# DeltaNet and a multiplicative FFN on one core: two more units' w1/w2 products from eleven half products, with the order of the second half written anew

## The chip, the core and the metric

The kernel runs on one core of a Trainium2 chip: TensorE (PE, matmuls into PSUM), VectorE (DVE), ScalarE (ACT), GpSimd (POOL) and SyncE (SP, which issues the DMAs). The metric is device time in microseconds, the median of several executions.

## The reference, cut to what matters

```python
# attention: q, k, v of (4, 8, 768, 48), beta of (4, 8, 768)
k_n = k / (norm(k) + 1e-06)
for t in range(768):
    y[t]  = q[t] @ state
    state = state + beta[t] * outer(k_n[t], v[t] - state.T @ k_n[t])
x = y as (4 * 768, 8 * 48)                   # 3072 tokens of 384 features
# ffn: w1, w2 of (384, 1024), w3 of (1024, 1024), w_out of (1024, 384)
out = (((x @ w1) * (x @ w2)) @ w3) @ w_out
```

All of it is float32.

## The kernel before, in words

The 768 positions are cut into 12 chunks of 64. Two chunks of all four batches, 512 tokens, are a **unit**; there are six, u = 0 to 5, and "the fourth unit" is u = 3. The delta rule is solved chunk by chunk: scores (step names `s`), the inverse of a triangular 32 x 32 block for every head (`V`, one run for two chunks), the corner that joins two such blocks (`e`), the state chain (`c`) and the outputs (`y`), which write the unit's transposed token features into the tile xT. The FFN folds w3 @ w_out once into one matrix w34. After that a unit has two stages: `a`, the products with w1 and w2 and their elementwise product, and `o`/`x`, the product with w34 and the results.

Nothing is scheduled by the machine: the table ORDER names one step after the other, each step is a piece of a generator (up to its next `yield`), and every engine executes its instructions in exactly that order. `a32` is a step of unit 3's pair (or slab) 2, `V4` one of the inverse for chunks 8 and 9, `S3` the sums over unit 3's slabs, `W` sums over w1 and w2, `X4` sums over unit 4's tokens, `n` and `g` GpSimd work on values and keys, `p` and `d` the loads and transposes of keys and queries, `N` the norms, `u` the write of a chunk's block to DRAM from which V loads it.

**Stage a of units 0 to 4** (`ab`, line 927): for each 128 of the 1024 FFN features, a **slab** of 128 x 512, three matmuls of 512 columns with w1 (384 features are 3 times 128), a copy to SBUF on ScalarE, three with w2, a multiplication on VectorE that reads the second product from PSUM.

**Stage a of the last unit, u = 5** (`features`, line 1055): two slabs at a time, as a **pair** p = 0 to 3, with 256 tokens per half. The 2 x 2 block scheme of Strassen and Winograd, with [w1 w2] as one operand and the unit's token halves as the other, needs seven products in place of eight for two thirds of the features; the last third takes four plain ones. That makes eleven products, each two matmuls of 256 columns (`onto`, one per slab of the pair), where the plain way has twelve of that size. They accumulate in four PSUM banks, ps_a to ps_d. ScalarE copies four intermediate sums out (into `first`, `tmp`, Y0, Y1), VectorE adds a bank to each of these four (line 1083), and Y0 \*= first and Y1 \*= tmp end the pair (lines 1118 and 1131): on VectorE for the last unit, on GpSimd for any other. Two sums over weights (T2, T3, T4 and a new w2, made by `W`, line 1020) and four over tokens (`X`, line 1043, on GpSimd) come first.

**Stage o** (`o`, line 1143) works on token halves and feature halves in seven blocks; between them GpSimd forms sums of the slabs in place (`slab_sums`, line 992).

**The inverse** (`inverse`, line 497) has 31 steps of two VectorE instructions, each on what the one before wrote: tb = V's column times U's row (line 524), V -= tb (line 529). From the third run on, V, U and tb all lie in SBUF.

PSUM banks are handed out in turn (`bank`, four of them): the fifth request gets the first again and its writer waits for that bank's last reader.

Of the kernel before, what the change touches and what calls it, by code (L numbers as in the profile page):

```python
# [45 lines left out]
P17 P17 f5 f5 V0 V0 f1 V0 V0 P17 t8 P15 V0 h0 V0 V0 P14 f5 P26 t6 P23 P20 V0 q2 P27 k2 t6 t9 t14
t9 v0 V0 P23 f4 f4 t14 f4 t15 t15 P21 P15 P15 t7 q3 V0 v1 Q2 Q2 V0 e0 h0 h0 e0 Q2 g1 e0 g1 t7 g1
f3 e0 e0 K2 P27 K2 e1 e0 e0 n0 e1 k3 f7 P27 n0 e1 c0 e1 P21 e1 f7 V1 g1 c0 y0 P28 c0 P20 P25 f7
P20 P20 P29 f3 P33 y0 n1 n1 P21 g1 c0 c1 y0 g1 g1 K2 f3 P28 P28 P28 P34 c1 t13 t13 t12 t12 P25
P27 K3 K3 K3 e1 s2 g1 P25 P29 P35 g1 P25 P33 f6 f6 P29 P29 e1 g1 N1 Q3 Q3 c1 y0 s2 s2 s2 P34 c1  # L50
s2 s2 f6 Q3 s3 K2 P30 P34 P34 P26 P26 P24 y1 y1 s3 P30 P31 N1 P33 N1 s3 b6 b6 P33 P35 P35 u2 P35
# [1307 lines left out]
```

## Time and profile before

| | before |
|---|---|
| time, median of 3 (us) | 558.43 (557.59 to 558.78) |
| span of the profiled execution (us) | 556.1 |
| granted TensorE clock | 1.000 |
| TensorE busy (us, share of the span) | 533.6 (96%) |
| VectorE busy | 343.7 (62%) |
| GpSimd busy | 169.7 (31%) |
| ScalarE busy | 145.7 (26%) |

The page gives the profiled execution by its span, from the first instruction to the last; the time of a whole execution is not given for it and lies 2.3 us higher in the median. A matmul in float32 leaves two records. A line number belongs to the kernel before; in the changed kernel the same code stands 10 to 16 lines lower. A group's row has the line, engine, operation, tiles and count, then busy us and mean ns, then the idle time before it and who ended it.

### The profile page before, as it was taken

The page shows a single profiled execution, that of the slowest core. Times are in us where ns is not written, and L with a number is a line of the kernel's source. Part 1 is how long each engine was busy: PE and PEld are TensorE (multiplying, and loading weights), DVE is VectorE, ACT ScalarE, POOL GpSimd, SP SyncE. Part 2 cuts the span into 40 slices and gives each one's busy share as a digit, 9 for nine tenths or more (in the row PEclk, how much of TensorE's full clock was granted, in tenths as well). Part 3 has the DMA queues.
Part 4 walks back from the last instruction along what each step waited for, and adds up shares of the span by engine and source line. Part 5 has one row for each costly group of instructions (what it writes and reads, how often), then busy time and mean ns, then how long its engine had stood idle before and what let it go on. Part 6 is the DMA issues. An engine that isn't in the chain of part 4 may idle for free.

```text
span 556.1 us, 19932 instructions
## 1 busy us (share of the span) xinstructions
PE 533.6 (96%) x8732; PEld 390.8 (70%) x8732; DVE 343.7 (62%) x800; ACT 145.7 (26%) x291; POOL 169.7 (31%) x213
## 2 busy tenths in 40 slices
...
GB/s 189 339 307 230 158 140 150 128 160 55 96 48 55 119 147 72 67 88 89 122 74 100 70 91 80 126 38 83 51 15 154 26 60 38 18 58 1 0 2 57
DMA packets 191527, 54.22 MB, mean 98 GB/s; under 512 B 178928, under 2 KB 185072, under 8 KB 191440
## 3 DMA queue, kind: packets, MB, share of 16 engines
...
q10 hardware_dynamic: 2112, 0.39, 0.5%
...
## 4 chain that ended last, share of the span: by engine, by line
PE 93%; DVE 3%; issue 2%; DMA 2%; ACT 0%; SPq 0%; DVEq 0%
PE ps_f L934 38%; PE ps_f L1166 20%; PE ps_f L913 7%; PE ps_w L672 6%; PE ps_w L777 4%; PE ps_f L1074 4%; PE ps_w L619 3%; PE ps_w L1074 2%; PE ps_w L451 2%; PE ps_f L369 1%; PE ps_w L457 1%; PE ps_f L904 1%; DMA beta_fm<-in_beta_dram 1%; PE ps_w L409 1%; PE ps_w L1166 1%
## 5 line engine op out<-in xcount | busy, mean ns | idle before, releaser
L934 PE MATMUL ps_f<-xT,w2s 128*128 128x512 f32 (+1 forms) x288 | 106.9, 524 | 0.0
L934 PE MATMUL ps_f<-xT,w1s 128*128 128x512 f32 (+1 forms) x288 | 106.7, 524 | 0.0
L934 PEld LDWEIGHTS ps_f<-xT,w2s 128*128 128x128 f32 x288 | 54.1, 190 | 46.5 <-issue 41.6
L934 PEld LDWEIGHTS ps_f<-xT,w1s 128*128 128x128 f32 x288 | 54.0, 190 | 45.3 <-issue 41.6
L1007 POOL TENSOR_TENSOR ab<-ab 128x256 f32<-128x256 f32 x80 | 56.4, 731 | 78.7 <-DVE ab L950 73.8
L946 ACT COPY ab<-ps_f 128x512 f32<-128x512 f32 (+1 forms) x48 | 24.3, 515 | 134.4 <-PE ps_f L934 130.3
L1166 PE MATMUL ps_f<-w,ab 128*128 128x192 f32 x320 | 57.3, 332 | 1.9 <-DVE osb L1197 1.3
L1166 PEld LDWEIGHTS ps_f<-w,ab 128*128 128x128 f32 x320 | 51.6, 190 | 3.3 <-issue 2.4
L524 DVE TENSOR_TENSOR tb<-Vb,Ub 128x31 f32<-128x31 f32 (+15 forms) x124 | 43.0, 347 | 15.4 <-DMA Ub<-Ud 11.5
L529 DVE TENSOR_TENSOR Vb<-Vb,tb 128x31 f32<-128x31 f32 (+15 forms) x124 | 43.0, 346 | 4.3
L913 PE MATMUL ps_f<-wo,w3T 128*128 128x384 f32 x128 | 43.5, 491 | 0.4 <-ACT w3T L907 0.4
L1166 PE MATMUL ps_f<-room,ab 128*128 128x192 f32 x240 | 42.8, 332 | 0.0
L950 DVE TENSOR_TENSOR ab<-ab,ps_f 128x512 f32<-128x512 f32 (+1 forms) x48 | 27.4, 589 | 24.0 <-PE ps_f L934 24.0
L1166 PEld LDWEIGHTS ps_f<-room,ab 128*128 128x128 f32 x240 | 38.7, 190 | 0.7
L913 PEld LDWEIGHTS ps_f<-wo,w3T 128*128 128x128 f32 x128 | 23.5, 190 | 15.4 <-ACT w3T L907 0.5
L301 POOL TENSOR_TENSOR sq<-ktok 128x384 f32<-128x384 f32 x24 | 19.7, 835 | 43.5 <-DMA out_dram<-osb 16.9
L658 POOL TENSOR_TENSOR vtok<-vtok,n 128x384 f32<-128x384 f32 x24 | 19.8, 832 | 39.5 <-DMA vtok<-in_v_dram 39.5
L635 ACT COPY T<-ps_w 32x512 f32<-32x512 f32 x24 | 13.8, 577 | 67.2 <-PE ps_w L619 46.2
L795 ACT COPY xT<-ps_w 112x256 f32<-112x256 f32 x48 | 14.3, 384 | 65.0 <-PE ps_w L777 61.7
L451 PE MATMUL ps_w<-KQ 48*64 48x128 f32 x320 | 21.9, 274 | 1.8 <-DVE PT L474 1.5
L717 DVE TENSOR_TENSOR X<-ps_w,wt 128x768 f32<-128x768 f32 x12 | 11.5, 956 | 19.4 <-PE ps_w L672 12.9
L1197 DVE TENSOR_TENSOR room<-room,ps_f 128x384 f32<-128x384 f32 (+1 forms) x13 | 7.0, 537 | 26.4 <-PE ps_f L1166 26.4
...
## 6 DMA issues: line engine op xcount, KB each, us to landing
...
Ud<-U SPq DMA_DIRECT2D x40, 64.0 KB, 2.8
...
```

What stands on the lines that cost most here:

```text
L451: pe.matmul(ps[half(z), 0, n : n + 128], lhsT=x[:, 0, :], rhs=x.rearrange("p j t -> p (j t)"), start=True, stop=True,)
L524: dve.tensor_tensor(out=tv, in0=V[:, 0 : s + 1, s : s + 1].to_broadcast([P, s + 1, n]), in1=U[:, s, s + 1 : BS].unsqueeze(1).to_broadcast( ...
L529: dve.tensor_tensor(out=o, in0=o, in1=tv, op=ALU.subtract)
L672: pe.matmul(out(ps, r, h, z), lhsT=lhs(r, h, z), rhs=rhs(r, h, z), start=True, stop=True,)
L777: i = pe.matmul(region(h, z, r), lhsT=lhs, rhs=rhs, start=part[n] not in part[:n], stop=part[n] not in part[n + 1 :],)
L913: pe.matmul(ps[:, 0:DM], lhsT=w3Ts[jc, kc // 4][:, kc % 4 * P : kc % 4 * P + P], rhs=wo(kc), start=(kc == 0), stop=(kc == KF - 1),)
L934: pe.matmul(ps[:].rearrange("p b c t -> p b (c t)"), lhsT=w[:, m, js], rhs=x[:, m, :, c0:c1].rearrange("p b c t -> p b (c t)"), start=(m = ...
L946: act.copy(out=t, in_=ps)
L950: dve.tensor_tensor(out=t, in0=t, in1=ps, op=ALU.mult)
L1007: (dve if u == last else pool).tensor_tensor(out=o_, in0=x_, in1=y_, op=op)
L1074: pe.matmul(ps[:, j, :], lhsT=w[j], rhs=x, start=first and j == 0, stop=j == 1, skip_group_check=not first,)
L1166: pe.matmul(ps[b][:, b, :], lhsT=ab_of(u, HF * f + i, t0), rhs=ws_[w][:, i], start=first and i == 0 and (b == 0 or n == "F"), stop=i == HF ...
```

## The change

**Units 3 and 4 use `features` too.** `LU`, the first unit that does, falls from 5 to 3. For these two units GpSimd does the two multiplications of a pair, all four banks come from the four that go in turn, and the sums of slabs are 8 of 128 x 512 instead of 16 of 128 x 256. `W`, which overwrites a third of w2, moves from the fifth unit to the time before the fourth; `X3` and `X4` are new.

**Room.** `first` and `tmp` no longer lie in a buffer of the keys and queries but in two of the ten slabs, Y0 and Y1 in eight fixed ones, S4 in a new tile `fourth`. T3 lies in qperm instead of kperm, and from chunk 10 on keys and queries are loaded into kperm one after the other. The inverse's tb has one buffer instead of two.

**Order.** The first 863 steps of ORDER are as before. Behind them the rows are new: 1382 steps became 1479.

The first place is TensorE where the fifth unit goes from its second to its third pair; before, from w1's to w2's products of two slabs. Before:

```order
L934 MATMUL ps_f<-xT,w1s 128x512 x3
L934 MATMUL ps_f<-xT,w2s 128x512 [waits Activation_49]
L934 MATMUL ps_f<-xT,w2s 128x512 x2
L934 MATMUL ps_f<-xT,w1s 128x512 [waits Activation_49]
L934 MATMUL ps_f<-xT,w1s 128x512 x2
L934 MATMUL ps_f<-xT,w2s 128x512 x3
```

Now:

```order
L1082 MATMUL ps_f<-xT,w2s 128x256 [waits Activation_49]
L1082 MATMUL ps_f<-xT,w2s 128x256
L1082 MATMUL ps_f<-xT,room 128x256 [waits DVE_49]
L1082 MATMUL ps_f<-xT,room 128x256
L1082 MATMUL ps_f<-xT,w1s 128x256 x2
L1082 MATMUL ps_f<-xT,w1s 128x256 [waits DVE_49]
L1082 MATMUL ps_f<-xT,w1s 128x256
L1082 MATMUL ps_f<-xT,w2s 128x256 x2
```

Three matmuls of 512 columns became single steps of two with 256. The row `xT,w1s` with a wait for DVE is the first product of pair three; it waits for the bank that VectorE adds into tmp of pair two.

The second place is VectorE in the fifth unit's inverse, V5. Before:

```order
L529 TENSOR_TENSOR Vb<-Vb,tb 128x20x12
L950 TENSOR_TENSOR ab<-ab,ps_f 128x512
L524 TENSOR_TENSOR tb<-Vb,Ub 128x231
L529 TENSOR_TENSOR Vb<-Vb,tb 128x21x11
L524 TENSOR_TENSOR tb<-Vb,Ub 128x220
L529 TENSOR_TENSOR Vb<-Vb,tb 128x22x10
```

Now:

```order
L540 TENSOR_TENSOR Vb<-Vb,tb 128x20x12
L1091 TENSOR_TENSOR first<-first,ps_f 128x512
L535 TENSOR_TENSOR tb<-Vb,Ub 128x231
L540 TENSOR_TENSOR Vb<-Vb,tb 128x21x11
L1091 TENSOR_TENSOR y_6083<-y_6083,ps_f 128x512
L535 TENSOR_TENSOR tb<-Vb,Ub 128x220
L540 TENSOR_TENSOR Vb<-Vb,tb 128x22x10
L1091 TENSOR_TENSOR tmp<-tmp,ps_f 128x512
L535 TENSOR_TENSOR tb<-Vb,Ub 128x207
L540 TENSOR_TENSOR Vb<-Vb,tb 128x23x9
```

The one multiplication among V5's steps became ten adds, one or two steps apart here. Over the first three pairs stand, ahead of pair two's tmp add, 14 of V5's steps, and 8 more ahead of pair three's; in the fourth unit 15 of V4's and 10 more.

The third place is GpSimd at the same time. Before, in the fourth and fifth unit:

```order
L1007 TENSOR_TENSOR ab<-ab 128x256 [waits PE_49] x2
L1033 TENSOR_TENSOR room<-w1s,room 128x256 [waits Pool_49]
L1033 TENSOR_TENSOR room<-w1s,room 128x256
L1037 TENSOR_TENSOR w2s<-w2s,w1s 128x512 [waits PE_49]
```

Now, in the fifth:

```order
L1060 TENSOR_TENSOR fourth<-xT 128x256 [waits Pool_49]
L1128 TENSOR_TENSOR y_5916<-y_5916,first 128x512 [waits DVE_49]
L1141 TENSOR_TENSOR y_5925<-y_5925,tmp 128x512 [waits DVE_49]
L1128 TENSOR_TENSOR y_5982<-y_5982,first 128x512 [waits DVE_49]
L1141 TENSOR_TENSOR y_6035<-y_6035,tmp 128x512 [waits DVE_49]
L1128 TENSOR_TENSOR y_6083<-y_6083,first 128x512 [waits DVE_49]
L1141 TENSOR_TENSOR y_6092<-y_6092,tmp 128x512 [waits DVE_49]
```

Before, GpSimd's next instruction behind the fourth unit's o stage waits for TensorE's products with w2; now GpSimd multiplies after every second add of VectorE, while V5 runs there.

The diff, with two of the table's rows:

```diff
 ORDER = """
...
-S2 e7 a21 e6 a23 a23 c6 e7 e7 c6 v7 o2 v9 o2 n7 n7 S2 y6 S2 S2 S2 V4 x2 K2 N4 c6 c6 o2 y6 e7 S2
...
+V4 V4 V4 X3 a30 a30 a30 a30 a30 a30 a30 a30 a30 V4 a30 a30 V4 V4 V4 V4 V4 V4 a31 a31 a31 a31
...
@@ -140,9 +145,9 @@
 
     turns, held = {}, set()
 
-    def in_turn(pool, shape, tag, n, name, dt=FP32):
-
-        i = turns.get(tag, -1)
+    def in_turn(pool, shape, tag, n, name, dt=FP32, at=None):
+
+        i = turns.get(tag, -1) if at is None else at - 1
         while True:
             i = turns[tag] = (i + 1) % n
             if (tag, i) not in held:
@@ -225,6 +230,9 @@
 
     ktoks, vtoks, KQs, PTs, Xs, Ss = {}, {}, {}, {}, {}, {}
 
+
+    LU, QM = 3, 10
+
     def load_crossed(src, m, dmas, tag, bufs):
 
         t = in_turn(work, [P, NR, H, D], tag, bufs, tag)
@@ -251,8 +259,11 @@
 
         return src.rearrange("(z r) h t d -> z (r h) t d", z=2)[z]
 
+    def perm_of_queries(m):
+        return qperm if m < QM else kperm
+
     def load_perm(m):
-        for src, dst in ((k, kperm), (q, qperm)):
+        for src, dst in ((k, kperm), (q, perm_of_queries(m))):
             for e in range(2):
                 for j in range(2):
                     nd = min(BS, D - BS * j)
@@ -349,7 +360,7 @@
 
     def by_vector(m):
         KQ = new_KQ(m)
-        for i, src in enumerate((kperm, qperm)):
+        for i, src in enumerate((kperm, perm_of_queries(m))):
             for z in range(2):
                 bs = slice(NR * z, NR * z + NR)
                 dve.transpose(
@@ -519,7 +530,7 @@
                 yield
         for s in range(BS - 1):
             n = BS - 1 - s
-            t = in_turn(work, [P, 256], "tb", 2, "tb")
+            t = in_turn(work, [P, 256], "tb", 1, "tb")
             tv = t[:, 0 : (s + 1) * n].rearrange("p (r t) -> p r t", t=n)
             dve.tensor_tensor(
                 out=tv, in0=V[:, 0 : s + 1, s : s + 1].to_broadcast([P, s + 1, n]),
@@ -816,8 +827,8 @@
     GUESTS = {10: "k", 2: "0", 9: "q", 18: "1", 19: "k", 11: "q", 14: "0", 15: "1", 26: "k", 21: "q", 32: "k", 34: "q"}
     spare = in_turn(work, [P, B, NP, 2, C], "KQ", 3, "spare")
 
-    def slab(name):
-        return in_turn(ffn, [P, CW], "slab", 10, name)
+    def slab(name, at=None):
+        return in_turn(ffn, [P, CW], "slab", 10, name, at=at)
 
     def guest(host):
         if host in "kq":
@@ -922,7 +933,11 @@
 
 
     last = NCH // 2 - 1
-    abs_ = {}
+    abs_, slots = {}, {}
+
+    def slot(x):
+        own = [slots[LU - 1, jc] for jc in range(KF)]
+        return (own + [i for i in range(10) if i not in own])[x]
 
     def ab(u, jc, c0, c1):
         x = xts[u]
@@ -942,6 +957,7 @@
         yield
         if (u, jc) not in abs_:
             abs_[u, jc] = slab("ab")
+            slots[u, jc] = turns["slab"]
         t = abs_[u, jc][:].rearrange("p (b t) -> p b t", b=B)[:, :, c0 * C : c1 * C]
         act.copy(out=t, in_=ps)
         yield
@@ -977,7 +993,7 @@
         ws_.update(T1=B12, T2=T2, T3=T3, T4=T4, B11=B11, B21=B21, B22=B22, M1=M1, U2=U2)
         ws_["U3"] = room[4][:, 0:DM]
         Ts["T2"] = room[4]
-        Ts["T3"] = kperm[:].rearrange("p b a x d -> p (b a x d)")
+        Ts["T3"] = qperm[:].rearrange("p b a x d -> p (b a x d)")
         Ts["T4"] = [x[:, HF * HD :] for x in room[:4]]
         for out_, x, y in ((T3, B22, B12), (B12, B12, B11), (T2, B22, B12), (T4, T2, B21)):
             for i in range(0, HF, 2):
@@ -1007,15 +1023,7 @@
                 (dve if u == last else pool).tensor_tensor(out=o_, in0=x_, in1=y_, op=op)
                 yield
 
-    LU = last
-    shared = []
-
-    def room_of_tokens():
-        if not shared:
-            x = in_turn(work, [P, B, NP, 2, C], "KQ", 3, "tsum")
-            x = x[:].rearrange("p b a j t -> p (b a j t)")
-            shared.extend((x[:, 0:CW], x[:, CW : 2 * CW], x[:, 2 * CW : 2 * CW + C * B]))
-        return shared
+    fourth = persist.tile([P, HB * P], FP32, name="fourth")
 
     def features_sums():
         n = CW
@@ -1047,7 +1055,7 @@
             (S3, A11, A21, ALU.subtract),
             (S1, A21, A22, ALU.add),
             (S2, S1, A11, ALU.subtract),
-            (room_of_tokens()[2], A12, S2, ALU.subtract),
+            (fourth[:], A12, S2, ALU.subtract),
         ):
             pool.tensor_tensor(out=out_, in0=x, in1=y, op=op)
             yield
@@ -1057,7 +1065,7 @@
         js = [slice((2 * p + j) * P, (2 * p + j + 1) * P) for j in range(2)]
         A11, A12, S1, A22 = (x_of(u, i % 2, i // 2) for i in range(4))
         S2, S3 = x_of(u, KM, 1), x_of(u, KM, 0)
-        tmp, first, S4 = room_of_tokens()
+        S4 = fourth[:]
         B11, B21, B31 = ([w1s[:, m, c] for c in js] for m in range(KM))
         T1, B22, B32 = ([w2s[:, m, c] for c in js] for m in range(KM))
         T2, T3 = ([Ts[x][:, c] for c in js] for x in ("T2", "T3"))
@@ -1085,16 +1093,18 @@
         ps_a = new()
         onto(ps_a, B11, A11, True)
         yield
+        first = slab("first", slot(8))[:]
         act.copy(out=both(first), in_=ps_a)
         yield
         ps_b = new()
         onto(ps_b, T1, S1, True)
         yield
+        tmp = slab("tmp", slot(9))[:]
         act.copy(out=both(tmp), in_=ps_b)
         yield
         onto(ps_a, T2, S2)
         yield
-        Y0 = both(slab("y0")[:])
+        Y0 = both(slab("y0", slot(2 * p))[:])
         act.copy(out=Y0, in_=ps_a)
         yield
         ps_c = new(True)
@@ -1106,7 +1116,7 @@
         yield
         onto(ps_a, T3, S3)
         yield
-        Y1 = both(slab("y1")[:])
+        Y1 = both(slab("y1", slot(2 * p + 1))[:])
         act.copy(out=Y1, in_=ps_a)
         yield
         onto(ps_b, B22, S4)
```

More of the change, by code (lines that the diff above doesn't have):

```diff
@@ L46 @@
[L46 to L51, printed above, removed]
@@ L76 @@
-c9 y8 y8 K1 S3 S3 c9 c9 o3 N5 o3 x3 s10 d11 s10 s10 y9 s10 s10 d11 d11 d11 S3 S3 W y9 y9 S3 S3
-o3 x3 W s10 x3 x3 s11 s11 s11 s11 s11 u10 u11 V5 S3 S3 x3 x3 o3 x3 x3 a44 s11 v11 V5 a45 V5 V5
-V5 V5 a45 a42 a42 v10 V5 a44 a46 a46 V5 V5 V5 V5 V5 V5 a41 V5 V5 V5 V5 a43 c9 a43 V5 V5 a41 a47
-a47 V5 V5 a44 a44 V5 V5 V5 V5 W V5 a40 a40 a45 V5 a43 V5 a41 V5 V5 V5 V5 a43 a45 a42 a40 a42 c9
-a46 V5 e10 e11 e10 W a41 W a40 c10 n10 n10 c10 e10 N5 a47 e10 e10 W a46 S4 a47 S4 S4 o4 S4 S4 S4
-e10 e11 e11 W x4 e11 c10 o4 S4 N5 e11 c10 c10 e11 c10 S4 S4 o4 x4 y10 S4 c11 n11 o4 S4 y10 n11
@@ L82 @@
[L82 to L87 removed]
+k0 g0 g0 g0 K0 V0 g0 k1 P12 K0 K0 beta K1 P0 g0 g0 K1 K1 g0 q1 P12 g0 P12 P12 beta g0 g0 beta
@@ new lines @@
+N0 P8 P9 P8 P8 P8 P3 P0 P3 P3 P9 P0 s1 s1 s1 P9 s0 P3 P0 P13 P13 P13 s0 s0 V0 V0 V0 P1 P1 Q1 P1
+P9 Q1 P10 P13 V0 V0 Q1 P1 P10 P2 P2 t0 t0 P2 P4 P4 V0 t1 P2 t1 V0 P4 P4 h1 t4 t4 N0 P6 f0 P7
+P10 P10 P5 t2 t5 P18 V0 V0 P11 P6 V0 P6 P6 N0 P16 P19 V0 P7 P7 P5 P5 P5 q0 V0 t5 h1 P18 f2 P11
+V0 P18 P7 t2 V0 f0 P14 h1 P22 P18 P19 f0 V0 P11 V0 V0 P11 P19 V0 V0 V0 P16 P16 P17 f2 f2 t10
+t10 P23 Q0 Q0 t3 P19 t11 V0 P16 Q0 V0 t3 P22 P22 P22 P14 V0 V0 V0 f1 V0 V0 P23 P21 t8 P15 f1
+P14 t11 P17 P17 f5 f5 V0 V0 f1 V0 V0 P17 t8 P15 V0 h0 V0 V0 P14 f5 P26 t6 P23 P20 V0 q2 P27 k2
@@ new lines @@
+t6 t9 t14 t9 v0 V0 P23 f4 f4 t14 f4 t15 t15 P21 P15 P15 t7 q3 V0 v1 Q2 Q2 V0 e0 h0 h0 e0 Q2 g1
+e0 g1 t7 g1 f3 e0 e0 K2 P27 K2 e1 e0 e0 n0 e1 k3 f7 P27 n0 e1 c0 e1 P21 e1 f7 V1 g1 c0 y0 P28
+c0 P20 P25 f7 P20 P20 P29 f3 P33 y0 n1 n1 P21 g1 c0 c1 y0 g1 g1 K2 f3 P28 P28 P28 P34 c1 t13
+t13 t12 t12 P25 P27 K3 K3 K3 e1 s2 g1 P25 P29 P35 g1 P25 P33 f6 f6 P29 P29 e1 g1 N1 Q3 Q3 c1 y0
+s2 s2 s2 P34 c1 s2 s2 f6 Q3 s3 K2 P30 P34 P34 P26 P26 P24 y1 y1 s3 P30 P31 N1 P33 N1 s3 b6 b6
+P33 P35 P35 u2 P35 s3 s3 s3 Q0 P30 P30 c1 b4 b4 P24 P24 u3 P24 y1 b5 b5 b5 V1 P26 y1 V1 b5 P31
@@ new lines @@
+V5 V5 a42 a42 a42 a42 a42 a42 a42 a42 a42 a42 a42 a42 a42 V5 a42 a42 V5 a42 a42 a42 a42 V5 a42
+a42 V5 V5 V5 V5 V5 V5 V5 V5 a43 a43 a43 a43 a43 a43 a43 c9 a43 a43 a43 a43 a43 a43 a43 a43 a43
+a43 o4 x4 v11 n11 c10 N5 N5 a43 a43 v10 n10 n10 c10 x3 V5 e10 S4 e10 e10 e10 e10 e10 a43 a43 S4
+S4 o4 e11 e11 e11 e11 S4 S4 c10 o4 S4 S4 x4 x4 S4 e11 e11 c10 c10 o4 y10 y10 c10 c11 o4 n11 c11
+c11 c11 y11 y11 y11 X5 X5 X5 x4 o4 x4 x4 o4 x4 x4 x4 x4 x4 a51 a50 a50 a50 a50 a50 a50 a50 a50
+a50 a50 a50 X5 a50 a50 a50 a50 a50 a50 a50 a50 a50 a50 a51 a51 a51 a51 a51 a51 a51 a51 a51 a51
```

68 lines of the change are left out of this document (33 added, 35 removed).

## The prediction

> **What bounds the kernel now.** I read the page's chain of waits first, then busy time by stretch, then the chain in order of time. The page's chain, by engine:
>
> ```profile
> PE 93%; DVE 3%; issue 2%; DMA 2%; ACT 0%; SPq 0%; DVEq 0%
> ```
>
> TensorE sets the time. The stretches view shows whether that also holds where the change works (columns: stretch, its length, busy time and count by engine, granted clock, DMA share, GB/s). The first two rows are the product stages of the fourth and fifth unit, the third is the sixth unit, already done the new way, the last runs from the third unit's last product to TensorE's end:
>
> ```profile
> core 0: us, PE busy (x) PEld busy (x) DVE busy (x) ACT busy (x) POOL busy (x), PEclk, DMA share, GB/s
> 342.59:388.84 46.25, 46.25 (x417) 21.98 (x417) 32.95 (x82) 8.07 (x14) 6.21 (x9) 1.00 0.44 88
> 420.42:464.64 44.22, 44.22 (x298) 20.34 (x301) 29.06 (x74) 5.64 (x10) 7.39 (x8) 1.00 0.40 76
> 496.29:534.35 38.06, 38.06 (x177) 33.35 (x177) 16.04 (x24) 9.18 (x16) 3.71 (x5) 1.00 0.03 10
> 309.57:552.60 243.03, 240.71 (x3597) 181.76 (x3596) 124.11 (x266) 41.01 (x84) 58.96 (x79) 1.00 0.27 52
> ```
>
> TensorE is idle for 2.32 us of the last 243, at full clock. So work taken from it counts in full, as long as nothing else starts to hold it. VectorE is what could: it is already two thirds busy in the first two rows, nearly all of it the inverse of two later chunks (V4, V5), while GpSimd is almost idle there. In the third row no inverse runs.
>
> **What the new products save.** The chain in order of time (start, us, what) gives both prices:
>
> ```profile
> 359.31 20.80 PE ps_f L934 x48
> ...
> 435.87 0.87 PE ps_w L672 x64
> ...
> 477.19 1.49 PE ps_w L777 x96
> 478.68 0.12 issue
> ...
> 500.61 1.73 PE ps_w L1074 x8
> ```
>
> A product leaves two records. One of 512 columns costs 20.80/48 x 2 = 0.867 us, one of 256 columns 1.73/8 x 2 = 0.432. A pair of slabs takes 12 of the former, 10.40 us, or 22 of the latter, 9.51 us. Eight pairs save 7.1 us. Two products ("one step" below) are 0.865.
>
> **What it adds.** Per unit VectorE gets 16 adds for 8 multiplications, ScalarE 16 copies for 8, and GpSimd 8 multiplications of 128x512, 8 sums of 128x512 for 16 of 128x256, and 4 token sums. The groups and single lines that price them (mean ns, or min/median/max):
>
> ```profile
> L1083 DVE TENSOR_TENSOR y<-y,ps_f x4: 687/687/689, 505.0 to 531.9; 128x512 f32<-128x512 f32 x4
> L1088 ACT COPY tsum<-ps_f x4: 586/586/587, 497.2 to 525.7; 128x512 f32<-128x512 f32 x4
> L1028 POOL TENSOR_TENSOR room<-kperm,w1s x2: 1272/1280/1287, 412.2 to 459.9; 128x512 f32<-128x512 f32 x2
> L717 DVE TENSOR_TENSOR X<-ps_w,wt 128x768 f32<-128x768 f32 x12 | 11.5, 956 | 19.4 <-PE ps_w L672 12.9
> PE ps_f L1166 <- DVE osb L1197: 1.3, 1, 1.3
> ```
>
> ScalarE (16 x 0.59 = 9.4 us in 38) hides. GpSimd has 8 x 1.28 + 8 x 1.28 + 4 x 0.73 = 23.4 us a unit, by itself no bound either. The weight sums (W), moved ahead of the fourth unit, fall into the 33 us of the third unit's output and state work, with W's last sums some 3 us before the product that reads them. The slabs reused for first, tmp and y are free because the o blocks that read them stand ahead on TensorE itself, and the single tb buffer orders two instructions of VectorE that wait for each other anyway. The last two chunks' queries now share the keys' buffer, and so load only after the keys' transposes:
>
> ```profile
> L261 SPq DMA_DIRECT2D kperm<-in_k_dram x64: 312/487/1851, 122.6 to 388.1; - x64
> ...
> kperm<-in_k_dram SPq DMA_DIRECT2D x32, 64.0 KB, 2.6
> ```
>
> Eight issues of about half a microsecond and 2.6 to land make some 6.6 us; for chunk 11, the tighter one, c9's R and X and the norms N5 fill some 8.5 on VectorE. I cost it at nothing; without that cover up to 2 us of o3 would be late. VectorE is the question, since the four banks a pair uses are used again by the next pair: TensorE's first product of a pair waits until VectorE has added the bank of the pair before into tmp, and V steps stand ahead of that add. The V steps, and how an add fits between two of them:
>
> ```profile
> 348.74 0.19 DVE L524 TENSOR_TENSOR tb<-Vb,Ub 128x31 f32<-128x31 f32 x1 [1.23 <-DMA Ub<-Ud]
> ...
> 355.89 0.40 DVE L529 TENSOR_TENSOR Vb<-Vb,tb 128x231 f32<-128x231 f32 x1
> ...
> 359.02 0.42 DVE L524 TENSOR_TENSOR tb<-Vb,Ub 128x255 f32<-128x255 f32 x1
> ...
> 359.94 0.43 DVE L524 TENSOR_TENSOR tb<-Vb,Ub 128x256 f32<-128x256 f32 x1
> ...
> 366.19 0.38 DVE L524 TENSOR_TENSOR tb<-Vb,Ub 128x207 f32<-128x207 f32 x1
> ...
> 368.54 0.32 DVE L524 TENSOR_TENSOR tb<-Vb,Ub 128x156 f32<-128x156 f32 x1
> ...
> 371.85 0.21 DVE L529 TENSOR_TENSOR Vb<-Vb,tb 128x31 f32<-128x31 f32 x1
> ...
> 443.71 0.41 DVE L529 TENSOR_TENSOR Vb<-Vb,tb 128x240 f32<-128x240 f32 x1
> 444.03 0.68 DVE L950 TENSOR_TENSOR ab<-ab,ps_f 128x512 f32<-128x512 f32 x1
> 444.63 0.39 DVE L524 TENSOR_TENSOR tb<-Vb,Ub 128x231 f32<-128x231 f32 x1
> ```
>
> The 31 steps run 348.74 to 372.06, 23.3 us, each bound by the one before. The first 14 take 10.28, the first 15 11.20, steps 15 to 22 7.17 (to 366.19), 16 to 25 8.60 (to 368.54), the last 9 5.87. An add between two steps costs 0.5: 0.60 to the next start, less 0.13 that it overlaps its predecessor.
>
> In both stretches of before GpSimd stands still beside V. Now its multiplications fall into it. Two lone GpSimd instructions of before did too:
>
> ```profile
> 270.01 0.95 POOL L301 TENSOR_TENSOR sq<-ktok 128x384 f32<-128x384 f32 x1 [16.94 <-DMA out_dram<-osb]
> 274.84 0.83 POOL L301 TENSOR_TENSOR sq<-ktok 128x384 f32<-128x384 f32 x1 [3.88 <-DVE Vb L529]
> ```
>
> ```profile
> 270.31 0.90 DVE L529 TENSOR_TENSOR Vb<-Vb,tb 128x231 f32<-128x231 f32 x1
> ...
> 274.86 1.09 DVE L524 TENSOR_TENSOR tb<-Vb,Ub 128x256 f32<-128x256 f32 x1
> ```
>
> The V instructions under them took 0.90 and 1.09 us where the same shapes take 0.40 and 0.43 above: 0.50 and 0.66 lost, 0.17 to 0.33 less than the GpSimd instruction's 0.83. An operation with one operand in PSUM does not suffer; this S update started inside a GpSimd sum and took its usual 0.95:
>
> ```profile
> 219.35 0.74 POOL L1007 TENSOR_TENSOR ab<-ab 128x256 f32<-128x256 f32 x1 [60.82 <-DVE ab L950]
> ```
>
> ```profile
> 219.19 0.94 DVE L738 TENSOR_TENSOR S<-S,ps_w 112x768 f32<-112x768 f32 x1
> ```
>
> So a multiplication of 1.28 us that meets V costs VectorE between 0 (if such meetings were chance) and 1.28; by the two rows 0.95 to 1.1, and I take 1.0. [...]
>
> **The fifth unit**, from its first product (0). V5 can start 8.8 us after U's last write (from the first row below to 348.74); that write ends about 1 us before 0, so V5 starts at 7.8. TensorE reaches pair three at 2 x 9.51 + 0.87 (chain step c9) = 19.9. Ahead of pair two's tmp add VectorE has 14 V steps (10.28) and 5 adds (2.5): 20.6, and with three multiplications met 23.6. TensorE waits 3.7 (0.7 without meetings). To pair three's tmp add: 8 steps, 4 adds, two meetings, 11.2 more, 34.8; TensorE is there at 33.1: 1.7 (0 without). Then 9 steps, an add, a meeting: V5 ends at 42.2.
>
> ```profile
> 339.25 0.68 DVE L463 TENSOR_TENSOR U<-ps_w,wt 128x512 f32<-128x512 f32 x1
> ...
> 452.00 0.21 DVE L529 TENSOR_TENSOR Vb<-Vb,tb 128x31 f32<-128x31 f32 x1
> ...
> 458.21 0.71 DVE L602 STREAM_TRANSPOSE T<-TT 128x512 f32<-128x512 f32 x1 [1.67 <-DMA TT<-Vd]
> ```
>
> ```profile
> 461.85 1.18 ACT L635 COPY T<-ps_w 32x512 f32<-32x512 f32 x2 [16.58 <-PE ps_w L619]
> ```
>
> After V's end the corner's transposition ends 6.7 us later (452.2 to 458.9), at 48.9; TensorE arrives at 48.3 (34.8 + 13.5 of products, o4 and c10): 0.6. e10's second products now stand right behind its first, with ScalarE's two copies between: 1.2 idle. Fifth unit: 7.2 us (1.9 without meetings).
>
> **The fourth unit** the same way: V4 starts at 6.7. Ahead of pair two's tmp add: 15 steps, 7 adds, 2.5 of meetings: 24.1; TensorE at 22.3 (o2's last block, with a bank wait of 1.3 - 0.87 = 0.4, lies between): 1.8. To pair three's: 10 steps, 4 adds, one meeting, 11.7; TensorE 10.4: 1.3. Pair four's third bank: 6 steps, an add and 2.3 of meetings (n8 and a square among them), 6.3, against 5.4: 0.9. Corner e8: 0.8 and 0.4. Together 5.6 us (0.8 without meetings).
>
> Elsewhere y9 and y11 now follow directly on the X they read: X's 0.96 + 0.1 less the third of 1.49 that doesn't read it: 0.5 each, 1.0 (o blocks stood between before). o4's last block waits 1.3, as the same block of the fifth unit does now.
>
> Sum: waits 5.6 + 7.2 + 1.0 + 1.3 = 15.1. Of today's 2.32 idle, six waits like the 0.12 row stay; the rest, 1.6, is replaced. Net +13.5 - 7.1 = +6.4 us: span 562.5. The page gives only that span, 556.1, for the profiled execution; the median is 2.3 above and I keep that difference: 564.8.
>
> **Rivals.** (1) The meetings cost nothing: waits 0.8 + 1.9 + 1.0 + 1.3 = 5.0, net 3.4 - 7.1 = -3.7, 554.7. For it: only two meetings are seen. Against: both show the loss, and no other V instruction of the four later inverses is long. (2) Nothing waits anew: -7.1, 551.3, at best -8.7 with today's 1.6 filled. Against: with free VectorE time the fifth unit's tmp add is still 0.7 late. (3) The far side: the meetings hold GpSimd as well, up to 0.4 (one V instruction) for each of its 16 multiplications; then first and tmp come free late for ScalarE's copies, the sums of o3 and o4 follow late, and each meeting takes the full 1.28: 2.5 + up to 4 us, 567 to 571. It decides once a GpSimd multiplication ends after the next pair's third step. (4) The change not doing what it says is excluded for the count: the order shows 88 products a unit; a higher price for 256 columns is excluded by the 1.73 row.
>
> **How the numbers follow.** Forecast 0.63, rival 1 0.20, rival 2 0.09, rival 3 0.08. The predicted time is the first's, 564.8; its own range is 560.5 to 569.5 (a meeting at 0.6 to 1.28). The range reaches from rival 1 with a us of slack, 553.5, to 570. A measurement here tells 0.2%, 1.1 us: slower takes the forecast and rival 3 less a little, 0.67; same, between rival 1 and forecast, 0.07; faster 0.26.
>
> **What would show it.** In the changed kernel: V instructions of 1.2 to 1.5 us where GpSimd's multiplication runs beside them, V4 and V5 stretched to about 35 us; TensorE idle before the first product of pairs three and four, released by VectorE's tmp add; 256-column products at 0.216 a record. The prediction is wrong if V instructions keep 0.4 us beside GpSimd, or if TensorE is idle under 6 us from the third unit's last product to its end.

## The result, and the profile after

| | before | changed |
|---|---|---|
| time, median (us) | 558.07 (556.17 to 559.16, 6 runs) | 572.63 (568.82 to 574.48, 6 runs) |
| span of the profiled execution | 556.1 | 570.9 |
| TensorE busy (us, share of the span) | 533.6 (96%) | 533.3 (93%) |

The change makes the kernel slower: ratio 1.0251, 95% interval 1.0224 to 1.0278. One execution of the kernel before, 908.86 us long at a granted clock of 0.567, is left out of every comparison here and below. Forecast was 564.8, with a range of 553.5 to 570. In the profiled execution the span grew by 14.8 us where +6.4 was forecast. The changed kernel's chain of waits, by engine:

```profile
PE 78%; DVE 11%; issue 6%; DMA 2%; POOL 1%; ACT 1%; SPq 0%; DVEq 0%; POOLq 0%; ACTq 0%
```

VectorE's share rose from 3% to 11%. To see where the time went, both spans are cut at the third unit's last product and at the sixth unit's first; "the stretch" below is what lies between. The stretches view of the changed kernel, then of the kernel before:

```profile
312.55:510.67 198.12, 182.14 (x3469) 160.31 (x3469) 119.80 (x242) 39.97 (x82) 80.17 (x84) 1.00 0.32 60
510.67:549.09 38.42, 38.42 (x180) 33.44 (x179) 16.13 (x24) 9.19 (x16) 2.69 (x4) 1.00 0.04 11
```

```profile
309.57:496.12 186.55, 184.28 (x3309) 130.33 (x3309) 99.34 (x226) 30.87 (x66) 55.08 (x75) 1.00 0.34 64
496.12:534.35 38.23, 38.23 (x179) 33.52 (x178) 16.04 (x24) 9.18 (x16) 3.88 (x5) 1.00 0.04 11
```

3.0 of the 14.8 us lie ahead of the change's first step (312.55 against 309.57), 11.6 in the stretch, 0.2 behind it. In the stretch TensorE's busy time fell by 2.1 us only, and its idle time rose from 2.3 to 16.0. The waits of TensorE there (engine, tile and line, what ended the wait, total us, times, longest):

```profile
PE ps_f L1082 <- DVE tmp L1091: 6.3, 5, 2.7
PE ps_f L1176 <- DVE osb L1207: 1.8, 2, 1.3
PE ps_w L630 <- DVE T L613: 1.7, 2, 0.9
PE ps_w L683 <- issue: 1.3, 1, 1.3
PE ps_w L788 <- DVE X L728: 1.2, 2, 0.7
...
PE ps_w L788 <- issue: 0.8, 1, 0.8
```

(The products and adds of lines 1074 and 1083 in the kernel before stand 8 lines lower here, at 1082 and 1091.) The first row is the wait that the prediction named: a pair's first product for VectorE's add into tmp. Its cause is in the order of time. GpSimd in the fourth unit, and VectorE's instructions beside it:

```profile
356.68 1.32 POOL L1141 TENSOR_TENSOR y<-y,tmp 128x512 f32<-128x512 f32 x1 [1.25 <-DVE y L1091]
364.59 1.38 POOL L1128 TENSOR_TENSOR y<-y,first 128x512 f32<-128x512 f32 x1 [6.59 <-DVE y L1091]
```

```profile
356.91 1.31 DVE L540 TENSOR_TENSOR Vb<-Vb,tb 128x192 f32<-128x192 f32 x1
358.25 0.37 DVE L535 TENSOR_TENSOR tb<-Vb,Ub 128x207 f32<-128x207 f32 x1
...
363.83 0.68 DVE L1091 TENSOR_TENSOR y<-y,ps_f 128x512 f32<-128x512 f32 x1
364.43 0.42 DVE L535 TENSOR_TENSOR tb<-Vb,Ub 128x255 f32<-128x255 f32 x1
364.88 1.37 DVE L540 TENSOR_TENSOR Vb<-Vb,tb 128x255 f32<-128x255 f32 x1
366.17 0.68 DVE L1091 TENSOR_TENSOR tmp<-tmp,ps_f 128x512 f32<-128x512 f32 x1
```

A V step under a multiplication takes 1.31 and 1.37 us instead of 0.36 and 0.42: 0.95 lost each. It ends 0.2 to 0.3 us after GpSimd does (358.00 and 358.22, 365.97 and 366.25). Over the eleven multiplications that met a V step the loss is 0.4 to 1.1 us, smaller the later the step starts under one. GpSimd's 1.27 grows to 1.39 at most. The tmp add behind it releases TensorE. The fourth unit's pair three, then the fifth unit's pairs three and four:

```profile
364.47 1.03 PE L1082 MATMUL ps_f<-xT,w1s 128*128 128x256 f32 x4
366.90 1.13 PE L1082 MATMUL ps_f<-xT,w1s 128*128 128x256 f32 x4 [1.40 <-DVE tmp L1091]
367.87 1.03 PE L1082 MATMUL ps_f<-xT,w2s 128*128 128x256 f32 x4
368.82 0.94 PE L683 MATMUL ps_w<-X,ktok 64*48 64x48 f32 x64
369.69 1.13 PE L1082 MATMUL ps_f<-xT,room 128*128 128x256 f32 x4
370.66 1.89 PE L1082 MATMUL ps_f<-xT,w1s 128*128 128x256 f32 x8
...
452.04 1.13 PE L1082 MATMUL ps_f<-xT,w1s 128*128 128x256 f32 x4 [2.68 <-DVE tmp L1091]
...
463.11 1.13 PE L1082 MATMUL ps_f<-xT,w1s 128*128 128x256 f32 x4 [1.19 <-DVE tmp L1091]
```

These rows also show what a wait costs beyond its idle time. Two products take 0.86 us from start to start in a row of products (the next kind starts 1.72 behind the x8 row), but 0.97 behind a wait and 0.95 to 0.97 beside another kind of work. And 364.47 plus 0.86 is 365.33, while the next could start at 366.90: 1.57 lost with 1.40 shown as idle.

### The profile page after: what moved, and what is told of

The parts are those of the page before. It is cut to its first block, busy times and chain, and to the rows that moved or that the text cites. A ratio compares the mean times of both kernels' runs of the same rounds, so it can differ in the third digit from the quotient of the medians.

```text
span 570.9 us, 20327 instructions
## 1 busy us (share of the span) xinstructions
PE 533.3 (93%) x8892; PEld 422.6 (74%) x8892; DVE 363.7 (64%) x816; ACT 154.8 (27%) x307; POOL 194.1 (34%) x221
## 4 chain that ended last, share of the span: by engine, by line
PE 78%; DVE 11%; issue 6%; DMA 2%; POOL 1%; ACT 1%; SPq 0%; DVEq 0%; POOLq 0%; ACTq 0%
PE ps_f L949 22%; PE ps_f L1176 19%; PE ps_f L1082 9%; PE ps_f L924 7%; PE ps_w L683 5%; PE ps_w L788 4%; DVE tb L535 3%; DVE Vb L540 3%; PE ps_w L630 3%; PE ps_w L1082 2%; PE ps_w L462 2%; PE ps_w L468 1%; PE ps_f L380 1%; PE ps_f L915 1%; DVE y L1091 1%
## 5 line engine op out<-in xcount | busy, mean ns | idle before, releaser
L949 PE MATMUL ps_f<-xT,w1s 128*128 128x256 f32 (+1 forms) x192 | 64.4, 488 | 0.0
L949 PE MATMUL ps_f<-xT,w2s 128*128 128x256 f32 (+1 forms) x192 | 64.2, 487 | 0.0
L1023 POOL TENSOR_TENSOR ab<-ab 128x256 f32<-128x256 f32 x48 | 33.7, 729 | 80.9 <-DVE ab L966 75.8
L949 PEld LDWEIGHTS ps_f<-xT,w1s 128*128 128x128 f32 x192 | 36.1, 190 | 24.1 <-issue 21.0
L1082 PE MATMUL ps_f<-xT,w1s 128*128 128x256 f32 x144 | 36.2, 384 | 7.1 <-DVE tmp L1091 6.3
L962 ACT COPY ab<-ps_f 128x256 f32<-128x256 f32 (+1 forms) x32 | 15.1, 479 | 81.6 <-PE ps_f L949 81.6
L1082 PE MATMUL ps_f<-xT,w2s 128*128 128x256 f32 x144 | 35.5, 380 | 0.0
L1176 PE MATMUL ps_f<-w,ab 128*128 128x192 f32 x192 | 34.2, 332 | 0.9 <-DVE tb L535 0.5
L924 PEld LDWEIGHTS ps_f<-wo,w3T 128*128 128x128 f32 x128 | 23.5, 190 | 15.5 <-ACT w3T L918 0.6
L312 POOL TENSOR_TENSOR sq<-ktok 128x384 f32<-128x384 f32 x24 | 19.7, 832 | 41.2 <-DMA out_dram<-osb 23.9
L1176 PE MATMUL ps_f<-w,y 128*128 128x192 f32 x184 | 32.3, 329 | 1.3 <-DVE osb L1207 1.3
L1176 PEld LDWEIGHTS ps_f<-w,ab 128*128 128x128 f32 x192 | 31.0, 190 | 1.9 <-POOL xT L1060 0.8
L1176 PEld LDWEIGHTS ps_f<-w,y 128*128 128x128 f32 x184 | 30.0, 190 | 2.0 <-issue 1.6
L1176 PE MATMUL ps_f<-room,ab 128*128 128x192 f32 x144 | 27.6, 347 | 0.0
```

What stands on the lines that cost most here:

```text
L312: pool.tensor_tensor(out=sq[:], in0=kt[:, r], in1=kt[:, r], op=ALU.mult)
L924: pe.matmul(ps[:, 0:DM], lhsT=w3Ts[jc, kc // 4][:, kc % 4 * P : kc % 4 * P + P], rhs=wo(kc), start=(kc == 0), stop=(kc == KF - 1),)
L949: pe.matmul(ps[:].rearrange("p b c t -> p b (c t)"), lhsT=w[:, m, js], rhs=x[:, m, :, c0:c1].rearrange("p b c t -> p b (c t)"), start=(m = ...
L962: act.copy(out=t, in_=ps)
L1023: (dve if u == last else pool).tensor_tensor(out=o_, in0=x_, in1=y_, op=op)
L1082: pe.matmul(ps[:, j, :], lhsT=w[j], rhs=x, start=first and j == 0, stop=j == 1, skip_group_check=not first,)
```

## The experiments

All kernels below were timed beside the kernel before, at 557.9 to 558.1 us (556.4 beside the one that ran once). The table gives the profiled stretch of each; the sections say what was edited.

| kernel | time | ratio to before (95%) | stretch | TensorE busy in it | idle |
|---|---|---|---|---|---|
| before, again | 558.47 | 1.0005 (0.9987 to 1.0023) | 186.99 | 184.75 | 2.2 |
| changed, again | 570.55 | 1.0234 (1.0215 to 1.0253) | 198.89 | 183.85 | 15.0 |
| without multiplications | 562.63 | 1.0090 (1.0056 to 1.0124) | 190.68 | 181.11 | 9.6 |
| writing only | 560.80 | 1.0063 (1.0044 to 1.0081) | 188.65 | 180.82 | 7.8 |
| without multiplications and adds | 559.71 | 1.0041 (1.0017 to 1.0065) | 187.86 | 180.52 | 7.3 |
| multiplications on VectorE | 572.93 | 1.0287 (1.0257 to 1.0317) | 201.41 | 185.79 | 15.6 |
| two o blocks moved | 575.78 | 1.0335 (1.0288 to 1.0382) | 205.50 | 187.27 | 18.2 |
| two other o blocks moved | 570.27 | one run | 198.97 | 184.08 | 14.9 |
| before, with squarings on GpSimd | 567.18 | 1.0183 (1.0154 to 1.0212) | 196.60 | 187.10 | 9.5 |
| before, with half products | 561.50 | 1.0071 (1.0041 to 1.0101) | 189.94 | 185.09 | 4.9 |

**The multiplications left out.**

```diff
-        (dve if u == last else pool).tensor_tensor(out=Y0, in0=Y0, in1=both(first), op=ALU.mult)
+        if u == last:
+            dve.tensor_tensor(out=Y0, in0=Y0, in1=both(first), op=ALU.mult)
```

(and the same for Y1)

> Changed kernel with GpSimd's 16 multiplications of the fourth and fifth unit left out (two of each pair; the slabs then hold the plain sums, so this part of the computation is missing). Theory A (they hold VectorE's V instructions, 1.0 us a meeting): no V instruction over 0.6 us beside them, V4 and V5 some 28 us long instead of 35, TensorE's waits at the first products of pairs three and four fall from 1.4, 0.7, 2.7 and 1.2 us to 0.3 or less each; by the prediction's sums 5.6 -> 0.8 and 7.2 -> 1.9, so 562.5 us instead of 572.6. Rival B (VectorE is late by its adds and V steps alone): V4 and V5 stay near 35 us and the time within 1.5 us of 572.6.

Measured 562.63 (560.17 to 563.47). Of the four waits at first products two are gone; 0.29 and 1.24 stay, the second at the fifth unit's pair three. The row of these waits in the stretch fell from 6.3 us to

```profile
PE ps_f L1082 <- DVE tmp L1091: 1.5, 2, 1.2
```

V4 and V5 take 30.7 and 30.3 us, longer than the 28 I expected, since other GpSimd work (values, squares, a slab sum) still meets them, for some 1.5 and 1.9 us. Theory A holds and B falls. That the time itself met A's 562.5 is in part luck: the stretch fell by 7.4 us (198.12 to 190.68) of the 10.1 that A takes off, and the other 2.6 of the profiled span lie ahead of the change's first step, where the changed kernel's first profile had lost 3.0 on its own (below). Against the changed kernel's second measurement, 570.55, the difference in time is 7.9.

**The meeting by itself, in the kernel before.**

```diff
         act.copy(out=t, in_=ps)
+        if u in (3, 4):
+            half_ = abs_[u, jc][:, 0 : CW // (u - 2)]
+            pool.tensor_tensor(out=half_, in0=half_, in1=half_, op=ALU.mult)
         yield
```

> Kernel before, with one GpSimd multiplication put behind each slab's copy in the fourth unit (128x512, squares the slab in place) and the fifth (128x256, squares half of it): the result of these units is then another, nothing else is added. It measures the meeting by itself. Theory A: V4 stretches from 23.3 us by about 0.95 for each of the 6 or 7 multiplications that fall into it, to about 29.5; V5 from 23.6 by some 0.4 each (a 256-column one takes 0.74), to about 26; since V4's end sets the corner, the time grows by 5 to 8 us. Rival B (meetings are harmless): V4 and V5 stay within 0.5 us of 23.3 and 23.6, no V instruction over 0.6 us, time within 1 us of before. [...]

V4 went from 23.3 to 29.0 us, V5 from 23.8 to 27.0, the time to 567.18 (566.56 to 568.67). GpSimd and VectorE, in the fourth unit and in the fifth:

```profile
364.01 1.06 POOL L949 TENSOR_TENSOR ab<-ab 128x512 f32<-128x512 f32 x1 [1.49 <-ACT ab L946]
...
443.05 1.49 POOL L949 TENSOR_TENSOR ab<-ab 128x256 f32<-128x256 f32 x2 [4.54 <-ACT ab L946]
```

```profile
364.21 1.14 DVE L529 TENSOR_TENSOR Vb<-Vb,tb 128x256 f32<-128x256 f32 x1
365.38 0.42 DVE L524 TENSOR_TENSOR tb<-Vb,Ub 128x255 f32<-128x255 f32 x1
...
443.38 0.69 DVE L529 TENSOR_TENSOR Vb<-Vb,tb 128x231 f32<-128x231 f32 x1
444.11 0.70 DVE L524 TENSOR_TENSOR tb<-Vb,Ub 128x240 f32<-128x240 f32 x1
```

A squaring, which reads one slab, takes 1.04 to 1.13 us (the multiplication of two slabs 1.27 to 1.39) and costs V some 0.7; one of 256 columns, 0.6 to 0.85 long, costs 0.3 to 0.45. So a meeting costs VectorE GpSimd's duration less 0.3 to 0.4, about the V step's own time. The 9.2 us on the whole, more than the 5 to 8 expected, are two waits, 5.09 and 1.97, and a drop of TensorE's clock that begins in the first (below).

**Writing without reading.**

```diff
-        (dve if u == last else pool).tensor_tensor(out=Y0, in0=Y0, in1=both(first), op=ALU.mult)
+        if u == last:
+            dve.tensor_tensor(out=Y0, in0=Y0, in1=both(first), op=ALU.mult)
+        else:
+            pool.memset(both(first), 0.0)
```

(and tmp in Y1's place)

> Changed kernel with GpSimd's 16 multiplications of the fourth and fifth unit replaced by memsets of first and tmp (128x512, at the same places of the order; GpSimd writes SBUF but reads none; the multiplications are missing from the result). If it is GpSimd's reading that holds V, V instructions beside the memsets keep 0.2 to 0.43 us and the stretch from the third unit's last product to the sixth unit's first is that of the kernel without the multiplications, 190.7 us. If any GpSimd instruction holds V, each V instruction beside one is 0.6 us or more and the stretch is 2 to 4 us longer than 190.7.

```profile
359.94 0.53 POOL L1131 MEMSET first<- 128x512 f32 x1 [6.71 <-DVE first L1091]
...
373.72 0.90 POOL L312 TENSOR_TENSOR sq<-ktok 128x384 f32<-128x384 f32 x1
```

```profile
359.81 0.41 DVE L535 TENSOR_TENSOR tb<-Vb,Ub 128x252 f32<-128x252 f32 x1
360.25 0.42 DVE L540 TENSOR_TENSOR Vb<-Vb,tb 128x252 f32<-128x252 f32 x1
...
373.97 0.83 DVE L540 TENSOR_TENSOR Vb<-Vb,tb 128x156 f32<-128x156 f32 x1
```

Beside a memset V keeps its 0.41 and 0.42; beside the square of the keys, which reads, it takes 0.83 instead of 0.32. The stretch, 188.65, is even 2 us below that without any multiplication, where V5 met three other GpSimd instructions (30.3 us long, against 28.5 here). It is the reading that holds V.

**The adds left out as well.**

```diff
-            dve.tensor_tensor(out=o_, in0=o_, in1=ps, op=ALU.add)
+            if u == last:
+                dve.tensor_tensor(out=o_, in0=o_, in1=ps, op=ALU.add)
```

> Changed kernel with the 16 multiplications and also VectorE's 32 adds of the fourth and fifth unit left out (the slabs hold single products): VectorE then has V alone in the two stages. It shows what the half products save when nothing waits for VectorE. If a pair costs TensorE 9.51 us (the prediction's term), TensorE's busy time from the third unit's last product to the sixth unit's first falls from 182.2 to about 177.5 and the time to about 556. Rival C (the saving itself was too large: each half product that follows a wait or a change of kind costs about 0.1 us more, whatever VectorE does): busy time stays at 180 to 181, time about 559 to 560.

Busy time 180.52, time 559.71 (557.69 to 561.98). Rival C holds: with nothing left that waits for VectorE in the products, the change still wins only 3.8 us of busy time, and the stretch is 0.9 to 1.3 us longer than before. In this kernel a pair costs more than the prediction's 9.51 us even where nothing stands between its products: 9.63 from the fourth unit's pair two to its pair three.

```profile
352.02 1.89 PE L1082 MATMUL ps_f<-xT,w1s 128*128 128x256 f32 x8
...
361.65 1.89 PE L1082 MATMUL ps_f<-xT,w1s 128*128 128x256 f32 x8
```

Pairs with a chain step between their products take 9.69 and 9.83, the step's 0.87 taken off. So no better place for the multiplications alone can make this order pay.

**The multiplications on VectorE.** Both lines become `dve.tensor_tensor(...)`.

> Changed kernel with the 16 multiplications of the fourth and fifth unit on VectorE instead of GpSimd, same order. Each then takes some 0.65 us between two V steps instead of holding one for 0.95. Theory A: V4 and V5 about 33 instead of 35 us, time 2 to 4 us below the changed kernel, 569 to 570.5. Rival B (meetings are harmless): VectorE has 16 x 0.65 more to do ahead of the adds TensorE waits for, time 4 to 8 us above, 577 to 580.

572.93 (572.36 to 574.58): neither. V4 takes 33.6 us, V5 34.9 (34.8 and 34.0 in the changed kernel, where A expected 33 here for both). The profiled stretch is 3.3 us longer than the changed kernel's, but TensorE ran at half clock for some 11 us of it (448 to 452 and 475 to 483), worth 5 to 6; without them it would be some 2 us shorter, an estimate, as A has it. The time itself tells the two apart no further than that.

**Half products in the kernel before.**

```diff
-            for m in range(KM):
+            for z in ((slice(0, 2), slice(2, 4)) if u in (3, 4) else (slice(0, B),)):
+                for m in range(KM):
```

(with `ps[:, z]` and `x[:, m, z, c0:c1]` in the matmul)

> Kernel before, with each matmul of 512 columns in the fourth and fifth unit's products cut into two of 256 (one token half after the other, into the same bank; same result, nothing else changed, and hardly any change of kind or new wait among them). It measures the price of a half product by itself. If the two rows of the prediction's price are right (0.867 for one of 512, 2 x 0.432 for two of 256), TensorE's busy time from the third unit's last product to the sixth unit's first stays within 0.5 us of 184.3 to 184.8 and the time within 1 us of before. If a half product as such costs more (a weight load for every 256 columns), and that is where the saving fell short, the busy time grows by 2 us or more.

Busy time 185.09, against 184.28 and 184.75 before: the price of a half product holds. Yet the time is 561.50 (559.90 to 565.09), and the stretch 3 us longer. This I had not expected. Two stalls in the middle of rows of short matmuls hold nearly all of it:

```profile
401.57 0.48 PE L777 MATMUL ps_w<-KQ,S 48*48 48x64 f32 x18 [0.99 <-issue]
...
482.02 0.45 PE L672 MATMUL ps_w<-S,KQ 48*64 48x48 f32 x15 [1.66 <-issue]
```

**What the stalls are.** The changed kernel has two of the same kind:

```profile
407.49 0.66 PE L788 MATMUL ps_w<-KQ,S 48*48 48x64 f32 x31
408.90 0.25 PE L788 MATMUL ps_w<-KQ,S 48*48 48x64 f32 x1 [0.76 <-issue]
...
496.70 0.26 PE L683 MATMUL ps_w<-S,KQ 48*64 48x48 f32 x2 [1.34 <-issue]
```

In the middle of a group, with no releaser. The stretches view counts TensorE's matmuls up to each: first the changed kernel, then the kernel before with half products.

```profile
0.00:408.90 408.90, 385.08 (x6963) 290.61 (x6963) 277.97 (x648) 125.10 (x247) 163.12 (x192) 1.00 0.58 117
0.00:496.70 496.70, 464.84 (x8363) 360.30 (x8364) 334.56 (x770) 143.48 (x285) 191.17 (x217) 1.00 0.53 106
```

```profile
0.00:401.57 401.57, 384.57 (x6964) 292.78 (x6965) 269.96 (x643) 120.40 (x239) 139.51 (x175) 1.00 0.59 120
0.00:482.02 482.02, 462.97 (x8365) 363.37 (x8365) 315.14 (x754) 134.06 (x269) 165.46 (x208) 1.00 0.53 109
```

Two programs with different work there stall at the same matmul of their list, the 6963rd and the 8363rd. In the kernel before, the 6963rd lies in an o block (402.72 to 405.50), and nothing shows. To see whether it is the supply of instructions, two o blocks were put ahead of the short rows (`c9 c9 y8 y8 o3` became `c9 c9 o3 y8 y8`, `c10 c11 o4` became `c10 o4 c11`):

> Changed kernel with two o blocks moved one place forward: an o3 block ahead of y8 instead of behind it, and an o4 block ahead of c11's first matmuls instead of behind them. TensorE stalled in the middle of y8 (0.67 to 0.93 us, at its 6963rd matmul) and of c11 (0.64 to 1.49, at the 8363rd) in every profile of the changed kernel and its variants, with nothing that it waited for. If its instructions arrive late there, because two or three hundred short matmuls stand in a row, the block of 2.8 us ahead gives them time: both stalls vanish or fall under 0.3 us. If something in y8 and c11 themselves is late, they stay. c11's second matmuls then follow directly on the first and wait for R instead, some 1.2 to 1.8 us, so the time is not expected to fall by more than 1 us.

Both stalls are gone (y8 and c11's first matmuls run through); the wait ahead of R's matmuls came, 1.18 us (the profile names no releaser for it, but it ends 0.11 us after VectorE's R), and one of 0.94 for the keys' sums of squares; 570.27 in one run. So y8 and c11 alone do not stall, nor does the place in the list; a row of short matmuls at that place does. My reading, that the instructions come late there, fits this, but no run shows it.

**The waits behind X, and o4's last block.** (`c9 c9 g5 g5 y9 y9 N5 p11 d11 o3` became `c9 c9 g5 g5 o3 y9 y9 N5 p11 d11`, and `x4 o4` went from behind y11 to ahead of it.)

> Changed kernel with two o blocks moved in the written order and nothing else: an o3 block ahead of y9, and o4's last block but one (with VectorE's step ahead of it) ahead of y11, so that y9 and y11 no longer follow directly on the X that they read and y11 lies ahead of o4's last block. If the prediction's terms of 0.5 + 0.5 + 1.3 us there are right, TensorE's waits of 0.54, 0.70 and 1.33 us at these places vanish and the stretch from the third unit's last product to the sixth unit's first shrinks by 2.2 to 2.6 us, time 570 to 570.5. If not, the waits move to the next block and the stretch stays within 0.5 us.

The three waits vanished where they were, and came back elsewhere:

```profile
503.01 2.84 PE L1176 MATMUL ps_f<-room,y 128*128 128x192 f32 x16 [1.70 <-DVE room L1207]
...
513.41 1.97 PE L1082 MATMUL ps_f<-xT,w1s 128*128 128x256 f32 x8 [2.49 <-DMA xT<-xT]
516.28 1.13 PE L1082 MATMUL ps_f<-xT,w2s 128*128 128x256 f32 x4 [0.91 <-POOL xT L1060]
```

The o4 block waits for the sum that stands behind X on VectorE, and y11's outputs, written some 4 us later behind c11, reach the sixth unit's first products late. In the fourth unit a wait of 1.17 us without a releaser, at the 7219th matmul, took y9's place ahead of the next scores. The time rose to 575.78 (573.65 to 579.91), some 5 us of it by two drops of the clock in the profiled run.

**Both kernels again, unchanged.**

> The kernel before, unchanged, to see whether TensorE's clock also drops in it. If the drops come with long waits of TensorE, the granted clock stays at 0.999 or 1.000 in nearly all runs, since it waits over 1.4 us only in the first 25 us; if they belong to the chip of that hour, some of these runs show 0.99 too. Third unit's last product at 309 to 310 us.

> The changed kernel, unchanged, again. If the 3.05 us that its first profile lost before the change's first step were that execution's own (a 0.93 us stall of TensorE and 3.5 us at half clock behind it), the third unit's last product ends at 309 to 310.5 us here; if they belong to the change (one tb buffer, more instructions to load), it ends at 312 to 313 again. The stretch from there to the sixth unit's first product stays at 198 us, longer by 1.5 to 2 for each drop of the clock in it. Granted clock below 0.998 in most runs, if the drops come with the waits.

The third unit's last product ended at 309.38 and 309.11 us: the 3.0 us of the first profile were that execution's own. There TensorE stalled for 0.93 us at 253.18 (0.33 at the same place before), and then its clock was halved until 257 (the clock is the third column from the end):

```profile
254.00:255.00 1.00, 1.00 (x5) 1.00 (x4) 0.53 (x1) 0.00 (x0) 0.00 (x0) 0.50 0.70 115
255.00:256.00 1.00, 1.00 (x5) 1.00 (x4) 0.00 (x0) 0.00 (x0) 0.00 (x0) 0.50 0.14 27
```

The second execution of the changed kernel had no drop there, but one behind the fifth unit's corner, where its waits stand close together:

```profile
474.04 0.76 PE L630 MATMUL ps_w<-T,U 33*33 33x32 f32 x64 [0.76 <-DVE T L613]
475.51 0.25 PE L630 MATMUL ps_w<-T,T 33*33 33x32 f32 x2 [0.71 <-ACT T L646]
476.11 0.74 PE L630 MATMUL ps_w<-T,T 33*33 33x32 f32 x62 [0.35 <-ACT T L646]
476.79 4.55 PE L1176 MATMUL ps_f<-room,y 128*128 128x192 f32 x16
```

That o block took 4.55 instead of 2.87 us: a drop costs 1.7. My expectation for the kernel before was wrong in its form: about half of its runs show a mean clock of 0.986 to 0.988. The profile puts that drop at 13 to 27 us, where TensorE stands idle for 1.5 and 4.1 us anyway, and it costs nothing that shows (spans 556.4 with it and 556.1 without). A drop of 3.4 us lowers the mean by 0.003 (the first profile, with that one drop, has 0.997). Of the other runs of the kernel before, all but two (0.994 and 0.997) show 0.999 or 1.000, so no drop; none of the ten runs of the changed kernel does: seven lie at 0.991 to 0.997, three at 0.985, the early drop and one more.

## Why the prediction was right and wrong

Taken from start to start, as the prediction did, against the changed kernel's first profile:

| step | forecast | measured |
|---|---|---|
| lost by a V step under a 128x512 multiplication | 1.0 | 0.95 in most |
| length of V4 and V5 | about 35 | 34.8 and 34.0 |
| fifth unit: pair two's third bank, pairs three and four, corner, its second half | 0, 3.7, 1.7, 0.6, 1.2 | 0.4, 2.8, 1.3, 0.9, 1.6 |
| fourth unit: o2's last block, pairs three and four, third bank, corner, its second half | 0.4, 1.8, 1.3, 0.9, 0.8, 0.4 | 0.6, 1.6, 0.9, 1.0, 1.1, 0.2 |
| y9, y11, o4's last block | 0.5, 0.5, 1.3 | 0.7, 0.9, 1.5 |
| sum of these waits | 15.1 | 15.5 |
| idle time of before that is replaced | -1.6 | -1.6 |
| stalls in y8 and c11, wait for R in c7 | 0 | 3.0 |
| saving by eleven products for twelve | -7.1 | about -5.3, what the rows above leave |
| stretch against before | +6.4 | +11.6 |

**What bounds the kernel**: right. VectorE holds TensorE at pairs three and four, by the tmp add, and GpSimd's multiplications make VectorE late. Leaving them out took 7.4 us off the stretch, where the prediction's sums give 10.1 without any meeting, and other GpSimd work still met V; rival 1 (meetings free) and rival 2 fall with it. Rival 3 falls as well: GpSimd itself is held for 0.12 us at most, and no run shows the full 1.28 a meeting from which it has its 2.5 us: the eleven meetings cost 0.4 to 1.1. The S update that the prediction cites began 0.16 us before the GpSimd sum (219.19 against 219.35), not inside it; it kept its usual 0.94 to 0.96 all the same.

**The waits** came out as forecast, to 0.4 us in the sum. That the sum is so close is in part luck: single terms miss by up to 0.9 us (3.7 against 2.8), in both directions. The fourth unit's first sum comes to 23.9 as it is written (6.7 + 11.2 + 3.5 + 2.5), not 24.1, which would have made its 1.8 the measured 1.6. The buffer that keys and queries share, costed at nothing, makes VectorE wait 0.4 us once and TensorE never. (c7's new wait of 0.3, which the first profile puts down to a load of keys, ends 0.05 us after VectorE's R, and the second profile names R.)

**The saving** is the term that was mis-sized: "A pair of slabs takes 12 of the former, 10.40 us, or 22 of the latter, 9.51 us." Both prices hold inside a row of products, and half products as such cost nothing more. But eleven products with other steps, waits and four banks between them break the row more often, and each break costs 0.1 us (0.95 to 0.97 for 0.86). With no adds to wait for, pairs took 9.63 to 9.83 us, by which eight pairs save 4.6 to 6.2. The step that failed here is rival 4's "a higher price for 256 columns is excluded by the 1.73 row": that row is four products on end, and prices no break. TensorE's busy time fell by 2.1 us; some 3 more are the edges of 15 new waits, at 0.2 each (8 waits fewer made 1.6 less busy time, 182.14 against 180.52), which the table counts as waits. The table's -5.3 is what the measured 11.6 leaves for the saving once the other rows are taken out; the missing 1.8 agrees with the pairs' rows but was not isolated by a run.

**Not in the sum at all**: the two stalls, some 2.5 with their edges, and c7's wait for R, some 0.5. The prediction had the rows to see that a stall without a releaser exists ("478.68 0.12 issue") and took six such for all there would be. It never asked what else could hold TensorE where the o blocks between short matmuls are taken away. And its range, built from the price of a meeting alone (0.6 to 1.28), left no room for this or for the saving.

**Beside the stretch**: the clock. It cost 1.7 us of the first profile (ahead of the change) and of the second (in the stretch). The granted clock falls to 0.50 there, for 3.4 us in both, and for up to 7 with the multiplications on VectorE. A long wait ahead of it did not decide it: the same wait of 2.7 us was followed by a drop in three profiles and by none in two others, while ahead of the second profile's drop stood no more than 0.76, 0.71 and 0.35 us close together, and 0.46 and 0.93 ahead of the first's. What sets a drop off no run shows. A forecast that adds waits should add 1.7 us for one such drop.

So the direction and the mechanism were right, the size was not: of the 8.4 us that the span missed, 3.0 were that execution's own, 3.0 the stalls and c7's wait, 1.8 the saving, 0.4 the waits and 0.2 the end. Measured again, without that execution's loss, the changed kernel took 570.55 us, still 5.8 more than the forecast.
